# Two chunks' key sums on GpSimd, one tile turned by DMA, and new lists for the first stage of a two-layer linear-attention kernel

## The chip, the cores and the metric

The kernel runs on one core of one Trainium2 chip. The metric is the device time of one execution in microseconds; it is compared as the median of several runs. All times below are microseconds unless marked ns.

## The reference

The input x has 2048 tokens of 512 features, in bfloat16. Two layers are applied; each is an attention block and an MLP block, both with a residual, and both layers use the same weights.

```python
def _A_ref(x, wqkv, wo):                       # 32 heads of 16 features
    q, k, v = qkv[0], qkv[1], qkv[2]           # from x @ wqkv
    phi = lambda t: jnp.where(t > 0, t + 1, jnp.exp(t)) + 1e-6
    pq, pk = phi(q), phi(k)
    kv = jnp.einsum("bhsd,bhse->bhde", pk, v)
    z = jnp.einsum("bhsd->bhd", pk)
    num = jnp.einsum("bhqd,bhde->bhqe", pq, kv)
    den = jnp.einsum("bhqd,bhd->bhq", pq, z)[..., None] + 1e-6
    return (num / den) ... @ wo
def _B_ref(x, w1, b1, w2, b2):                 # 512 -> 1792 -> 512
    return gelu(layernorm(x) @ w1 + b1) @ w2 + b2
x = x + _A_ref(_layernorm(x), A_wqkv, A_wo)
x = x + _B_ref(_layernorm(x), ...)             # and both once more
```

The change concerns z, the sum of phi(K) over all tokens, in the first layer.

## The kernel before

The 2048 tokens are 16 tiles of 128 tokens, numbered 0 to 15, in 4 chunks of 4 tiles. Names end in layer and tile (K0_14: layer one, tile 14) or in layer, chunk and part (Q0_3_2). The program makes a graph of named operations, and each of the five engines executes its own written list of names (CONF, ORDER: "pe" is TensorE, "act" ScalarE, "dve" VectorE, "pool" GpSimd, "sp" the queue that issues most DMAs). A planner walks through these lists with a cost for each operation; it gives out the buffers and PSUM banks in the order in which it sees operations start, and from that the program sets its semaphore waits. It does not change the order within a list. WAY, a second table, says for many operations on which engine or in which form they run.

The first stage of layer one takes the chunks in the order 3, 0, 1, 2. For each tile it does the following.

- Layer norm. statsA0 and aggrA0 (VectorE, L742, L744) give mean and variance; vepsA0 (mostly GpSimd, L755) and powA0 (GpSimd, L757) give rstd; nmrA0 (GpSimd, L774) is made for those tiles whose normA0 runs on ScalarE (L777); the other normA0 run on VectorE (L782). The tiles of chunk 3 are only centred (cenA0) and are scaled later (yscA0).
- Transposition. TA0 is a DMA transpose that SP issues (L792). Tiles 1, 12, 13, 14 and 15 are turned on TensorE instead (PTA0, L805), and ScalarE copies the result out of PSUM (tcA0, L815).
- K0 (TensorE, L860), then phi: expk0 and reluk0 (ScalarE, L830, L841), mink0 (VectorE, L834 or L843), phik0 (VectorE, L836 or L847; phik0_6 on GpSimd). Where the table says "max", there is no relu and phik0 reads PSUM itself.
- Q0 (L878, L891) with the same phi.
- G0 (L961): normed tile transposed times phi(K), summed over all 16 tiles in PSUM banks 0 to 3. K, Q, the PTA0, Z and D operations share banks 4 to 7 meanwhile.

z is made by attn_z. With ZC=(0, 3), layer one makes it on TensorE: for each chunk, Z0_c multiplies each of the 16 blocks of phi(K) by one column of ones (L942), and VectorE adds the result to zs (zs0_c, L948, L951). In layer two, whose entry is 3, three chunks go another way that the function also holds: tiles are added into zacc in float32 on GpSimd or VectorE (za1, L914), the sum is split into a high and a low bfloat16 part (zhi, zlo), and one block of eight one-column matmuls sums over the partitions (ZH, L930), from which zsh writes zs:

```python
            if n < cf["ZC"][L]:
                ...
                    on_pool = eng(f"za{L}_{st}") != "dve"
                    G.op("pool" if on_pool else "dve",
                         lambda e, second=second, k=k: e.tensor_tensor(
                             zacc[:], pkb[:, zfirst[L].slot, :] if second else zacc[:], pkb[:, pks[k].slot, :], op=ALU.add),
```

After the stage, zb0 puts zs on a block-diagonal mask, D0_c_k (L1085) makes the denominators, ln and rec (ScalarE, L1087, L1089) their reciprocals and pr0 (L1093) the products; for chunks 2 and 3 this is done by token (ZR0, cpz0, pz0, red0, den0, rec0, pr0). cpg0 copies G out of PSUM, KV0 (L1016) and kvm0 (L1035) make the masked product with wv, M0 (L1039) multiplies by wo, cpm0 copies, and WO0 (L1109) makes the attention's output. RA0 adds the residual; normB0, TB0 or PTB0 lead to the MLP, whose matmuls are W10 (L1141) and W20 (L1180).

GpSimd also issues the loads of the later weights (wv, wo, w1_0, w1_1, w2_0, w2_1, L682), which wait for all transposes of the stage. SP loads the biases b1 and b2; b1 is turned by a small DMA transpose (Tb1, L1239) and copied by ScalarE (b1c, L1240) for the gelu.

## Time and profile before

| | |
|---|---|
| median of 3 runs | 325.48 |
| lowest and highest | 325.1 and 325.51 |
| the profiled execution | 325.25 |
| its span in the trace | 323.5 |
| TensorE matmul, busy | 318.4 |
| VectorE, busy | 216.5 |
| ScalarE, busy | 195.0 |
| GpSimd, busy | 134.8 |
| granted TensorE clock | 1.0 |

The span is the time in the trace from the first to the last instruction; the device time of the same execution is 1.75 longer. In the page's strips, the span is cut into 40 slices of 8.1 each, and a digit is the busy share in tenths. In a timeline a row is: start, duration, engine, line, operation, output<-input, count, and in brackets the idle time before it. PEld is the weight load, which overlaps PE. The chain of waits puts 91% of the span on TensorE.

### The profile page before, as it was taken

Reading aid. Unit: us, or ns where it says so; the run is one execution under the profiler, and the core shown is the slowest. Engines: PE = TensorE matmul, PEld = TensorE weight load, DVE = VectorE, ACT = ScalarE, POOL = GpSimd, SP = SyncE. Lnnn points to the kernel's source line nnn. Section 1 sums busy time; section 2 is a strip of 40 time slices with the busy share of each in tenths; the row PEclk is TensorE's granted clock in tenths of the full one; section 3 lists DMA queues with packets and bytes.
Section 4 is the critical chain, followed back from the end, with each engine's and each line's share of the span. In section 5 each row is a group of like instructions: output and inputs, shape, how many; then the busy total and the mean of one; then the engine's idle time right before and its main releaser. Section 6 shows DMA issues by size and latency. Waiting matters only on the chain.

```text
span 323.5 us, 4765 instructions
## 1 busy us (share of the span) xinstructions
PE 318.4 (98%) x1698; PEld 159.9 (49%) x1729; DVE 216.5 (67%) x506; ACT 195.0 (60%) x336; POOL 134.8 (42%) x224
## 2 busy tenths in 40 slices
PE   8999999999999999999999999999999999999996
...
POOL 4673268638703359000266645763541754000000
...
DMA packets 47028, 20.39 MB, mean 63 GB/s; under 512 B 42076, under 2 KB 45532, under 8 KB 47004
## 3 DMA queue, kind: packets, MB, share of 16 engines
...
q8 instruction: 14, 0.23, 0.3%
q14 instruction: 10, 0.08, 0.1%
...
## 4 chain that ended last, share of the span: by engine, by line
PE 91%; DVE 7%; issue 1%
PE ps L1180 28%; PE ps L1141 26%; PE ps L860 8%; PE ps L1109 6%; PE ps L878 5%; PE ps L993 4%; PE ps L961 4%; PE ps L891 3%; DVE xsb L1114 2%; DVE stats L742 2%; PE ps L698 2%; DVE yb L782 1%; PE ps L1167 1%; DVE lr L1061 1%; PE ps L1085 1%; DVE rd L1064 1%
## 5 line engine op out<-in xcount | busy, mean ns | idle before, releaser
L1147 ACT ACTIVATE gT<-ps,b1c 128x512 bf16<-128x512 f32 (+1 forms) x140 | 77.0, 600 | 63.3 <-PE ps L1141 62.6
L1141 PE MATMUL ps<-t,w 128*128 128x512 bf16 (+1 forms) x556 | 101.2, 336 | 0.2
L1180 PE MATMUL ps<-w,gT 128*128 128x512 bf16 x424 | 97.6, 379 | 0.5
L1141 PEld LDWEIGHTS ps<-t,w 128*128 128x128 bf16 x560 | 54.7, 98 | 43.8 <-ACT t L815 0.3
L1180 PEld LDWEIGHTS ps<-w,gT 128*128 128x128 bf16 x434 | 42.5, 98 | 50.0
L757 POOL TENSOR_TENSOR rstd<-veps,neghalf 128x1 f32<-128x1 f32 x64 | 38.5, 612 | 5.2 <-DVE veps L755 3.1
L830 ACT ACTIVATE eb<-ps 128x512 bf16<-128x512 f32 x56 | 32.4, 600 | 13.1 <-PE ps L878 6.2
L1190 DVE TENSOR_TENSOR pkb<-ps,xsb 128x512 bf16<-128x512 f32 x15 | 10.1, 684 | 40.7 <-PE ps L1180 40.7
L742 DVE BATCH_NORM_STATS2 stats<-xsb 128x6 f32<-128x512 f32 x48 | 32.2, 677 | 0.3
L860 PE MATMUL ps<-wqkv,t 128*128 128x512 bf16 x125 | 31.1, 379 | 0.2
L1109 PE MATMUL ps<-gtb,t 128*128 128x512 bf16 x123 | 30.1, 379 | 0.3
L841 ACT ACTIVATE rb<-ps 128x512 bf16<-128x512 f32 x38 | 22.2, 601 | 8.9 <-PE ps L860 6.7
L747 POOL TENSOR_SCALAR veps<-mv 128x1 f32<-128x1 f32 x32 | 8.7, 272 | 44.6 <-DVE mv L744 42.2
L755 POOL TENSOR_SCALAR veps<-mv 128x1 f32<-128x1 f32 x28 | 7.2, 262 | 45.1 <-DVE mv L744 43.7
L777 ACT ACTIVATE yb<-xsb,nmr,rstd 128x512 bf16<-128x512 f32 x21 | 16.9, 810 | 11.6 <-POOL nmr L774 11.5
L782 DVE TENSOR_SCALAR yb<-xsb,mv,rstd 128x512 bf16<-128x512 f32 x27 | 14.8, 559 | 11.4 <-POOL rstd L757 11.2
L1186 DVE TENSOR_TENSOR xsb<-ps,xsb 128x512 f32<-128x512 f32 x16 | 10.9, 682 | 16.8 <-PE ps L1180 14.3
L843 DVE TENSOR_SCALAR eb<-eb 128x512 bf16<-128x512 bf16 x46 | 14.5, 329 | 7.8 <-ACT eb L830 7.6
L860 PEld LDWEIGHTS ps<-wqkv,t 128*128 128x128 bf16 x128 | 12.4, 98 | 14.6 <-ACT eb L830 0.3
L878 PE MATMUL ps<-wqkv,t 128*128 128x512 bf16 x76 | 19.4, 379 | 0.2
L1109 PEld LDWEIGHTS ps<-gtb,t 128*128 128x128 bf16 x128 | 12.4, 98 | 14.2 <-ACT gtb L974 0.5
L1126 POOL TENSOR_TENSOR xsb<-xsb,b2b 128x512 f32<-128x512 f32 x14 | 17.3, 1235 | 1.0 <-DVE yb L782 0.7
...
## 6 DMA issues: line engine op xcount, KB each, us to landing
...
t<-yb SPq DMA_TRANSPOSE x56, 2.5
...
t<-t SPq DMA_TRANSPOSE x20, 2.4
```

The source lines that it names most:

```text
L742: G.op("dve", lambda e: e.bn_stats(stats[:, s.slot, :], src()), 602, reads=src_keys, writes=[k + "s"], tiles=[s, *src_tiles], prio=prio, n ...
L757: G.op("pool", lambda e: e.tensor_tensor(rstd[:, s.slot:s.slot + 1], veps[:, s.slot:s.slot + 1], neghalf[:], op=ALU.pow), 530, reads=[k + ...
L782: G.op("dve", lambda e: e.tensor_scalar(yb[:, y.slot, :], src(), stats[:, s.slot, 2:3] if by_act else mv[:, s.slot, 0:1], rstd[:, s.slot:s ...
L830: G.op("act", lambda e: e.activation(eb[:, et.slot, :], bank(bt), ACT.Exp, scale=factor()), 569 if by else 483, reads=[src_key, *more], wr ...
L841: G.op("act", lambda e: e.activation(rb[:, rt.slot, :], bank(bt), ACT.Relu, scale=factor()), 569 if by else 478, reads=[src_key, *more], w ...
L860: ins = e.matmul(bank(b), lhsT=yTa(yT)[:, dt, k * P:(k + 1) * P], rhs=wqkv[:, dt, D:2 * D], start=(dt == 0), stop=(dt == DT - 1))
L878: ins = e.matmul(bank(b), lhsT=yTa(yT)[:, dt, k * P:(k + 1) * P], rhs=wqkv[:, dt, 0:D], start=(dt == 0), stop=(dt == DT - 1))
L1109: ins = e.matmul(bank(wb), lhsT=yTa(pq)[:, kt, k * P:(k + 1) * P], rhs=gtb[:, kt, :], start=(kt == 0), stop=(kt == DT - 1))
L1126: G.op("pool" if on_pool else "dve", lambda e: e.tensor_tensor(xsb[:, st, :], xsb[:, st, :], b2b[:], op=ALU.add), 1120 if on_pool else 600 ...
L1141: ins = e.matmul(bank(b, n), lhsT=w1[:, dt, ft * P:(ft + 1) * P], rhs=yTa(yT)[:, dt, k0 * P:k1 * P], start=(dt == 0), stop=(dt == DT - 1))
L1147: G.op("act", lambda e, ft=ft, b=b, k0=k0, k1=k1, n=n: e.activation(gT[:, g.slot, ft * 512 + k0 * P:ft * 512 + k1 * P], bank(b, n), ACT.Ge ...
L1180: ins = e.matmul(bank(b), lhsT=gT[:, g.slot, ft * 512 + k * P:ft * 512 + (k + 1) * P], rhs=w2[:, ft, :], start=(ft == 0), stop=(ft == FT - 1))
```

## The change

ZC becomes (2, 3): the first two chunks of layer one (chunks 3 and 0) take the other way through attn_z. Z0_3, Z0_0, zs0_3 and zs0_0 go; za0_13, za0_14, za0_15, za0_0, za0_1, za0_2, za0_3 (all on GpSimd, since the table does not name them), zhi0, zlo0, ZH0 and zsh0 come. Tile 1 of layer one is turned by DMA: PTA0_1 and tcA0_1 go, TA0_1 comes. The lists of all five engines are re-ordered between their first few operations and the first MLP of chunk 0, and are the same as before from there on: from W10_0_12_1 in TensorE's list, reluq0_2_2 in ScalarE's, aggrB0_6 in VectorE's, pz0_2_1 in GpSimd's, TB0_2 in SP's. One line more in a list moves the line numbers of the functions by one.

```diff
-    C0=(3, 0, 1, 2), N_WARM=8, ZC=(0, 3), LQ='sp', N_HALF=1, N_K=4, N_Q=3, P_Z0=6.15, N_PB=1, N_PT=8, P_DEN=-50.43,
+    C0=(3, 0, 1, 2), N_WARM=8, ZC=(2, 3), LQ='sp', N_HALF=1, N_K=4, N_Q=3, P_Z0=6.15, N_PB=1, N_PT=8, P_DEN=-50.43,
...
         "pe":
-            "warm PTA0_12 idle0_0 PTA0_13 K0_12 idle0_1 K0_13 PTA0_14 Q0_3_0 Q0_3_2 PTA0_15 G0_12_0 K0_14 K0_15 "
-            "Q0_3_3 Q0_3_1 G0_13_0 PTA0_1 G0_14_0 K0_0 Z0_3 G0_15_0 K0_1 K0_3 K0_2 Q0_0_2 Q0_0_3 G0_0_0 G0_1_0 Q0_0_0 "
-            "K0_8 G0_2_0 G0_3_0 K0_5 Z0_0 K0_4 K0_6 K0_7 Q0_0_1 K0_10 K0_11 Q0_1_0 K0_9 Q0_1_3 Z0_1 G0_4_0 Z0_2 "
-            "Q0_1_2 Q0_1_1 G0_5_0 D0_0_3 D0_0_0 G0_6_0 D0_0_1 G0_7_0 D0_0_2 G0_8_0 ZR0 G0_9_0 G0_10_0 G0_11_0 G0_11_2 "
-            "D0_1_0 G0_11_1 Q0_2_0 G0_11_3 KV0_0 D0_1_1 KV0_1 D0_1_2 KV0_2 KV0_3 Q0_2_1 M0_1 M0_2 M0_0 M0_3 Q0_2_2 "
-            "WO0_0_0 WO0_0_1 WO0_0_2 WO0_0_3 D0_1_3 WO0_1_0 WO0_3_0 WO0_2_0 Q0_2_3 WO0_5_0 WO0_4_0 WO0_6_0 PTB0_0 "
...
+            "warm PTA0_12 idle0_0 PTA0_13 K0_12 idle0_1 K0_13 PTA0_14 Q0_3_0 K0_14 PTA0_15 G0_12_0 Q0_3_2 K0_15 "
+            "Q0_3_3 G0_13_0 Q0_3_1 K0_0 G0_14_0 K0_3 G0_15_0 K0_1 G0_0_0 Q0_0_2 K0_2 Q0_0_3 Q0_0_1 G0_1_0 Q0_0_0 "
+            "G0_2_0 K0_8 K0_4 G0_3_0 K0_6 K0_5 K0_10 K0_7 G0_4_0 ZH0 K0_11 K0_9 Q0_1_3 Z0_1 Q0_1_0 Q0_1_1 Z0_2 G0_5_0 "
+            "Q0_1_2 D0_0_0 G0_6_0 G0_7_0 D0_0_1 D0_0_3 G0_8_0 D0_0_2 G0_9_0 G0_10_0 G0_11_0 G0_11_2 G0_11_1 D0_1_0 "
+            "Q0_2_0 G0_11_3 ZR0 D0_1_1 KV0_0 KV0_1 KV0_2 KV0_3 D0_1_2 D0_1_3 M0_2 M0_0 M0_3 M0_1 Q0_2_1 WO0_0_0 "
+            "WO0_0_1 WO0_0_2 WO0_0_3 WO0_1_0 WO0_2_0 Q0_2_2 WO0_3_0 WO0_5_0 WO0_6_0 Q0_2_3 PTB0_0 WO0_7_0 WO0_4_0 "
...
         "act":
-            "wk1 sumA0_13 tcA0_12 sqA0_13 tcA0_13 expk0_12 reluk0_12 tcA0_14 expk0_13 reluq0_3_0 reluk0_13 tcA0_15 "
-            "reluq0_3_2 expq0_3_0 expk0_14 reluk0_14 normA0_3 expq0_3_2 expk0_15 reluk0_15 reluq0_3_3 tcA0_1 yscA0_15 "
-            "expk0_0 expq0_3_3 reluq0_3_1 expq0_3_1 reluk0_1 expk0_1 normA0_5 normA0_8 expk0_2 reluq0_0_2 normA0_10 "
-            "reluk0_3 expq0_0_3 expk0_3 normA0_6 normA0_7 expk0_8 expq0_0_0 expq0_0_2 reluq0_0_0 reluk0_5 expk0_5 "
-            "expk0_4 normA0_9 reluk0_6 expk0_6 expk0_7 reluq0_0_1 expq0_0_1 expk0_10 expk0_11 reluk0_11 expk0_9 "
-            "reluk0_9 expq0_1_3 expq0_1_2 expq0_1_0 reluq0_1_2 expq0_1_1 ln0_0_0 rec0_0_0 ln0_0_1 rec0_0_1 ln0_0_3 "
-            "rec0_0_3 reluq0_1_1 cpz0 ln0_0_2 rec0_0_2 ln0_1_0 expq0_2_0 rec0_1_0 ln0_1_1 b1c rec0_1_1 cpm0_1 cpm0_0 "
-            "cpm0_3 ln0_1_2 rec0_1_2 ln0_1_3 rec0_1_3 expq0_2_1 expq0_2_3 reluq0_2_1 reluq0_2_3 expq0_2_2 tcB0_0 "
...
+            "wk1 sumA0_13 tcA0_12 sqA0_13 tcA0_13 expk0_12 reluk0_12 tcA0_14 reluk0_13 expk0_13 reluq0_3_0 tcA0_15 "
+            "expq0_3_0 reluk0_14 expk0_14 normA0_3 expq0_3_3 reluq0_3_3 expk0_15 yscA0_15 reluk0_15 expk0_0 "
+            "reluq0_3_2 expq0_3_2 expq0_3_1 normA0_10 reluq0_3_1 expk0_1 reluk0_1 normA0_8 reluk0_3 expk0_3 expk0_2 "
+            "reluq0_0_2 expq0_0_2 normA0_5 normA0_6 expq0_0_3 expq0_0_0 reluq0_0_0 normA0_7 expk0_8 reluq0_0_1 "
+            "expq0_0_1 expk0_4 normA0_9 expk0_6 reluk0_6 expk0_5 reluk0_5 expk0_7 expk0_10 expk0_11 reluk0_11 expk0_9 "
+            "reluk0_9 expq0_1_3 b1c expq0_1_0 expq0_1_1 ln0_0_0 expq0_1_2 rec0_0_0 reluq0_1_2 ln0_0_1 ln0_0_3 "
+            "rec0_0_1 rec0_0_3 reluq0_1_1 ln0_0_2 rec0_0_2 ln0_1_0 expq0_2_0 rec0_1_0 ln0_1_1 cpz0 rec0_1_1 cpm0_0 "
+            "cpm0_1 cpm0_3 ln0_1_2 rec0_1_2 ln0_1_3 rec0_1_3 expq0_2_1 reluq0_2_1 expq0_2_2 expq0_2_3 tcB0_0 "
+            "reluq0_2_3 gelu0_0_5_0 gelu0_0_8_0 gelu0_0_11_0 gelu0_0_0_0 gelu0_0_13_0 gelu0_0_12_0 gelu0_0_2_0 "
...
         "dve":
-            "statsA0_15 mink0_12 aggrA0_15 phik0_12 vepsA0_14 cenA0_15 statsA0_0 aggrA0_0 vepsA0_15 statsA0_3 "
-            "mink0_13 statsA0_1 aggrA0_3 normA0_0 phik0_13 statsA0_2 aggrA0_1 aggrA0_2 mink0_14 yscA0_13 statsA0_10 "
-            "normA0_1 yscA0_14 phik0_14 normA0_2 minq0_3_0 mink0_15 statsA0_5 phik0_15 phiq0_3_0 aggrA0_5 aggrA0_10 "
-            "minq0_3_2 statsA0_8 zs0_3 phiq0_3_2 aggrA0_8 mink0_0 statsA0_6 statsA0_4 statsA0_7 aggrA0_4 aggrA0_7 "
-            "aggrA0_6 phik0_0 statsA0_9 mink0_1 minq0_3_3 aggrA0_9 mink0_2 phik0_1 phik0_2 minq0_3_1 normA0_4 "
-            "statsA0_11 minq0_0_3 mink0_3 phiq0_3_3 phiq0_0_3 phik0_3 aggrA0_11 phiq0_3_1 mink0_8 phik0_8 minq0_0_0 "
-            "phiq0_0_0 normA0_11 mink0_5 mink0_4 zs0_0 phik0_5 phik0_4 mink0_7 minq0_0_2 mink0_6 phiq0_0_2 phik0_7 "
-            "mink0_10 mink0_11 phik0_10 minq0_0_1 mink0_9 phik0_11 phik0_9 zs0_1 minq0_1_3 zs0_2 zb0 phiq0_1_3 "
-            "phiq0_0_1 dz0 minq0_1_0 minq0_1_2 phiq0_1_0 pr0_0_0 minq0_1_1 pr0_0_1 pr0_0_3 cpg0_0 cpg0_1 cpg0_2 "
-            "cpg0_3 minq0_2_0 kvm0_2 kvm0_1 kvm0_0 kvm0_3 phiq0_2_0 cpm0_2 pz0_2_0 red0_2_0 RA0_0 statsB0_0 RA0_1 "
-            "statsB0_1 aggrB0_0 aggrB0_1 RA0_2 RA0_3 normB0_1 statsB0_2 normB0_0 RA0_4 aggrB0_2 statsB0_3 pz0_3_3 "
-            "den0_2_0 RA0_5 aggrB0_3 normB0_2 red0_3_3 rec0_2_0 normB0_3 RA0_6 pz0_3_1 pz0_3_0 pr0_2_0 minq0_2_3 "
...
+            "statsA0_15 mink0_12 aggrA0_15 phik0_12 vepsA0_14 cenA0_15 vepsA0_15 statsA0_3 statsA0_0 aggrA0_3 "
+            "aggrA0_0 statsA0_2 mink0_13 yscA0_14 phik0_13 normA0_0 yscA0_13 statsA0_1 aggrA0_1 mink0_14 aggrA0_2 "
+            "statsA0_10 phik0_14 normA0_1 minq0_3_0 aggrA0_10 statsA0_8 aggrA0_8 normA0_2 mink0_15 minq0_3_3 phik0_15 "
+            "phiq0_3_0 statsA0_5 mink0_0 aggrA0_5 phik0_0 statsA0_7 phiq0_3_3 statsA0_6 statsA0_4 aggrA0_7 aggrA0_4 "
+            "aggrA0_6 mink0_1 minq0_3_1 phik0_1 statsA0_11 phiq0_3_1 minq0_3_2 mink0_2 aggrA0_11 normA0_4 phik0_2 "
+            "statsA0_9 phiq0_3_2 mink0_3 aggrA0_9 minq0_0_3 phiq0_0_3 minq0_0_2 minq0_0_0 phik0_3 phiq0_0_2 mink0_8 "
+            "normA0_11 phik0_8 minq0_0_1 mink0_4 phiq0_0_1 zhi0 phik0_4 phiq0_0_0 zlo0 mink0_5 mink0_7 phik0_5 "
+            "mink0_6 zsh0 phik0_7 mink0_10 phik0_10 mink0_11 phik0_11 mink0_9 phik0_9 zs0_1 minq0_1_0 zs0_2 phiq0_1_0 "
+            "zb0 minq0_1_3 phiq0_1_3 dz0 minq0_1_1 pr0_0_0 minq0_1_2 pr0_0_1 pr0_0_3 cpg0_0 cpg0_2 cpg0_1 cpg0_3 "
+            "minq0_2_0 kvm0_2 kvm0_0 kvm0_3 kvm0_1 phiq0_2_0 cpm0_2 pz0_2_0 red0_2_0 RA0_0 RA0_1 statsB0_0 statsB0_1 "
+            "aggrB0_0 aggrB0_1 RA0_2 RA0_3 normB0_1 RA0_5 normB0_0 den0_2_0 statsB0_2 statsB0_3 aggrB0_2 rec0_2_0 "
...
         "pool":
-            "id0 bdm0 neghalf id1 bdm1 powA0_12 vepsA0_13 eps6 powA0_13 powA0_14 vepsA0_0 powA0_15 b1z powA0_0 "
-            "vepsA0_3 powA0_3 nmrA0_3 vepsA0_1 powA0_1 vepsA0_2 powA0_2 vepsA0_5 powA0_5 nmrA0_5 vepsA0_8 powA0_8 "
-            "vepsA0_10 powA0_10 nmrA0_10 nmrA0_8 vepsA0_7 vepsA0_4 powA0_7 powA0_4 vepsA0_9 vepsA0_6 powA0_6 powA0_9 "
-            "nmrA0_7 nmrA0_6 vepsA0_11 powA0_11 nmrA0_9 phik0_6 w1_1 phiq0_1_2 wv wo w2_1 phiq0_1_1 w1_0 pr0_0_2 "
-            "pr0_1_0 pr0_1_1 w2_0 pr0_1_2 pr0_1_3 vepsB0_1 powB0_1 vepsB0_0 powB0_0 b20_0 vepsB0_2 powB0_2 vepsB0_3 "
...
+            "id0 bdm0 neghalf id1 bdm1 powA0_12 vepsA0_13 eps6 powA0_13 b1z powA0_15 powA0_14 vepsA0_3 vepsA0_0 "
+            "powA0_0 powA0_3 nmrA0_3 za0_13 vepsA0_1 vepsA0_2 powA0_1 powA0_2 za0_14 vepsA0_10 vepsA0_8 powA0_10 "
+            "powA0_8 nmrA0_8 nmrA0_10 vepsA0_5 za0_15 powA0_5 za0_0 vepsA0_7 vepsA0_4 vepsA0_6 powA0_4 powA0_6 "
+            "nmrA0_5 nmrA0_6 za0_1 powA0_7 vepsA0_11 nmrA0_7 vepsA0_9 powA0_9 powA0_11 za0_2 nmrA0_9 za0_3 phik0_6 wv "
+            "w1_1 wo w1_0 w2_0 w2_1 phiq0_1_2 phiq0_1_1 pr0_0_2 pr0_1_0 pr0_1_1 pr0_1_2 pr0_1_3 vepsB0_1 powB0_1 "
+            "vepsB0_0 powB0_0 vepsB0_2 powB0_2 vepsB0_3 powB0_3 phiq0_2_3 b20_0 pz0_2_1 vepsB0_6 vepsB0_7 vepsB0_5 "
...
         "sp":
-            "x0 x1 wk0 x2 wq xc0 xc1 xc2 TA0_0 TA0_3 TA0_2 TA0_5 TA0_8 TA0_4 TA0_6 TA0_7 TA0_10 TA0_11 TA0_9 b1 b2 "
-            "Tb1 TB0_1 TB0_2 TB0_3 TP0_2_0 TB0_5 TB0_7 TB0_6 TB0_4 TP0_3_1 TP0_3_0 TP0_3_3 TP0_2_3 TP0_2_1 TP0_2_2 "
...
+            "x0 x1 wk0 x2 wq xc0 xc1 xc2 TA0_0 TA0_3 TA0_1 TA0_2 TA0_10 TA0_8 b1 TA0_4 TA0_6 TA0_5 TA0_7 TA0_11 TA0_9 "
+            "Tb1 TB0_1 b2 TB0_2 TB0_3 TP0_2_0 TB0_5 TB0_7 TB0_6 TB0_4 TP0_3_1 TP0_3_0 TP0_3_3 TP0_2_3 TP0_2_1 TP0_2_2 "
...
-        "TA0_0": "dma", "TA0_1": "pe", "TA0_10": "dma", "TA0_11": "dma", "TA0_12": "pe", "TA0_13": "pe", "TA0_14": "pe",
+        "TA0_0": "dma", "TA0_1": "dma", "TA0_10": "dma", "TA0_11": "dma", "TA0_12": "pe", "TA0_13": "pe", "TA0_14": "pe",
```

98 rows, old and new, of the table ORDER are left out of this document.

## Prediction

> **What bounds the kernel now.** I read the page first, then the PE timeline of the first stage, then the rows of what is removed and added.
>
> ```profile
> PE 318.4 (98%) x1698; PEld 159.9 (49%) x1729; DVE 216.5 (67%) x506; ACT 195.0 (60%) x336; POOL 134.8 (42%) x224
> ...
> PE   8999999999999999999999999999999999999996
> ...
> POOL 4673268638703359000266645763541754000000
> ```
>
> TensorE is busy from the second slice to the last. Busy includes pipelined waiting, so I also took the ends of the operations from the trace's semaphore posts: the n-th post of an engine belongs to the n-th name of its list. From 7 us on, posts follow each other at 0.864 us for four 512-column matmuls, and only G0_15 shows more (0.04 us). So any TensorE work taken out shortens the run, and any new wait lengthens it, microsecond for microsecond.
>
> ```profile
> 16.59 1.03 PE L860 MATMUL ps<-wqkv,t 128*128 128x512 bf16 x4
> 17.45 0.54 PE L942 MATMUL ps<-onesm,pkb 128*128 128x1 bf16 x16
> 18.09 0.81 PE L961 MATMUL ps<-pkb,yb 128*128 128x512 bf16 x3
> ```
>
> This is Z0_3, one of the two blocks to go, between K0_0 and G0_15: sixteen one-column matmuls.
>
> **What is removed and added on TensorE.** Z0_3 and Z0_0 post 0.38 us after their predecessors and push the next post by 0.02: 2 x 0.40 = 0.80 us. The transpose PTA0_1 is 0.22. ZH0 comes in; its twin ZH1 posts after 0.18 and pushes the next by 0.02: 0.20. Sum: 0.80 + 0.22 - 0.20 = 0.82 us less, if TensorE stays filled. Nothing hides this work today, so all of it counts. tcA0_1 (ScalarE, 0.48) goes too.
>
> **What GpSimd gets: seven adds.** Their rows are those of layer two's (L914):
>
> ```profile
> L914 POOL TENSOR_TENSOR zacc<-zacc,pkb x6: 1152/1248/1534, 166.0 to 187.1; 128x512 f32<-128x512 f32 x6
> L914 DVE TENSOR_TENSOR zacc<-zacc,pkb x4: 679/683/692, 165.3 to 174.1; 128x512 f32<-128x512 f32 x4
> ```
>
> 7 x 1.15 = 8.1 us at least, 8.7 at the median, put between the small operations that make rstd. GpSimd is busy 14.35 of the 27.5 us from 6.5 to 34, so it fits in sum. But each add stands before a nmr or pow that a norm waits for, and it holds VectorE:
>
> ```profile
> 34.14 1.26 POOL L847 TENSOR_TENSOR pkb<-eb,rb 128x512 bf16<-128x512 bf16 x1 [5.44 <-DVE eb L843]
> ```
> ```profile
> 35.05 0.50 DVE L834 TENSOR_SCALAR eb<-eb 128x512 bf16<-128x512 bf16 x1
> 35.65 0.29 DVE L843 TENSOR_SCALAR eb<-eb 128x512 bf16<-128x512 bf16 x1
> ```
>
> The short VectorE operation that starts at 35.05, inside the 1.26 us GpSimd add, ends 0.15 after the add does (35.40); the next one takes 0.29. So such an operation is held until the add ends. Statistics and operations that read PSUM are not held. Each add can cost VectorE between nothing and about 1.1 us.
>
> The Trainium skill (GPSIMD Engine Reference, Engine selection and Key points) speaks against this edit: it puts elementwise work on VectorE and says that GpSimd shares its memory interfaces with VectorE. The two L914 rows agree (1.248 against 0.683). If sharing only doubled a VectorE operation's time, 0.28 would be lost at each add instead of up to 1.1, and the sum below would come to about -0.6; the row at 35.05 shows a hold, so I use holds.
>
> **Where the adds bite, list by list.** TensorE starts on time if its operand is posted 0.24 before the previous post (G0_15 today has 0.19 and loses 0.04). Other lags from the posts: VectorE to GpSimd 0.13, GpSimd to VectorE 0.12, GpSimd to ScalarE 0.15, TensorE to ScalarE 0.14.
>
> First chain, to G0_15. cenA0_15 posts at 9.60 as now; vepsA0_15 9.66; powA0_15 +0.67; powA0_14 +0.53; vepsA0_3, vepsA0_0 to 11.45; powA0_0 +0.65; powA0_3 +0.53; nmrA0_3 +0.37 = 13.00; za0_13 +1.12 = 14.12. mink0_14 is held to 14.27; aggrA0_2 14.36; vepsA0_2 14.69; powA0_1 +0.65; powA0_2 +0.53; za0_14 +1.15 = 17.02. normA0_2 is held to 17.30; mink0_15, minq0_3_3, phik0_15 (0.20 + 0.20 + 0.33) = 18.03. With the new list TensorE comes to G0_15 at 18.28: wait 0. It has no slack left, though. phik0_0 follows at +1.82 (0.33 + 0.60 + 0.20 + 0.09 + 0.60) = 19.85 and is wanted 0.24 before 20.01: wait 0.08.
>
> Second chain, ScalarE. normA0_10, normA0_5 and normA0_9 stand in its list where their nmr, now behind a za, comes at 19.28, 24.80 and 30.40. ScalarE is free at 19.29, 24.83 and 30.48, so each wait is about 0.1. Adding 0.57 (scaled) or 0.49 for each exp or relu and 0.70 for each norm, expk0_3 posts at 23.36 (Q0_0_1 waits 0.06), reluq0_0_0 at 27.82 (K0_4 waits 0.14), reluk0_6 at 32.23 (K0_7 waits 0.09): PSUM banks 4 to 7 rotate among all of K and Q, and these posts free them.
>
> Third, the end of the sum. za0_3 ends at 31.55 and holds minq0_0_1 to 31.70; mink0_4, phiq0_0_1, zhi0, phik0_4 (0.20 + 0.33 + 0.34 + 0.60) = 33.17: G0_4 waits 0.07. phiq0_0_0 and zlo0 (0.93): ZH0 waits 0.07.
>
> Fourth, a wait that has nothing to do with GpSimd: M0_2 now stands two D matmuls (0.43) behind KV0_3, where Q0_2_1 (0.86) stood too. kvm0_2 posts 0.32 after KV0_3, and 0.24 more makes 0.56: wait 0.13. Then pr0_1_3 on GpSimd and normB0_0 before PTB0_0, 0 to 0.2, taken 0.05, because today's margin there is 0.36 and the new list shortens it.
>
> Sum of waits: 0.08 + 0.29 + 0.14 + 0.13 + 0.05 = 0.69. **Net -0.82 + 0.69 = -0.13 us.**
>
> Bounds. These waits are links of one 25 us chain. If it runs 2% quicker (0.5 us) than my roundings, all but 0.18 go; a chain this tight could also leave less than that. On the other side, small GpSimd operations are themselves slowed when VectorE runs beside them: powA0_3 today takes 0.91 from vepsA0_3 where 0.65 is usual, during phik0_13. Twice that, 0.5, and the median instead of the minimum for the adds (4 of 7 on the chain, 0.1 each, 0.4) make waits of 1.6, so +0.8.
>
> **Edits at nothing.** TA0_1 goes to the SP queue as a twelfth transpose: 1.2 us of issue, 2.55 to landing (12.41 to 14.95 for TA0_0). normA0_1 posts near 15.7, so it lands near 18.3; K0_1 starts at 19.1. Behind it, TA0_2 waits for normA0_2 (17.30) anyway. Cover: 0.8 us. The six weight loads now leave GpSimd back to back (0.8 to 0.95 us each) after phik0_6, ahead of phiq0_1_2, which is needed only near 43; wv is wanted at 48. b2 behind TB0_1 costs SP 0.4 us while the queue is empty.
>
> **Rivals.**
>
> *The lists close.* All operands come in time: -0.82 + 0.1 = 324.75. For it: today's list, equally tight, loses 0.04. Against: the seven holds are not there today.
>
> *GpSimd is the bound of the stage.* Every add is lengthened and small operations pile up behind: waits 1.6, time 326.3. It decides from the point where nmrA0_3 posts later than about 13.4, since the rest follows in series. For it: the zero slack at G0_15 and the 0.91 above.
>
> *Tb1 blocks ScalarE.* b1c moves from 50.6 to behind expq0_1_3, near 37.8, and everything for D0 stands behind it. Its transpose Tb1 waits for TA0_9 (lands about 34.6).
>
> ```profile
> t<-yb SPq DMA_TRANSPOSE x56, 2.5
> ...
> b1t<-b1r SPq DMA_TRANSPOSE x1, 6.7
> ```
>
> At 2.5 it lands at 37.2, in time. At the 6.7 of today's row, 41.4: ScalarE stands 3.6 us and TensorE some 3.4, time 328.7. Today Tb1 was issued at 35.56, beside w1_1 (35.44), whose packets came first on the engines; in the new order wv leaves about 1.5 us after Tb1. The Trainium skill (Trainium Kernel Development and Optimization, Key Constraints) says that all queues share the same 16 DMA engines; the row fits. It decides if Tb1 lands after 37.9.
>
> *The removed work was only filler.* If the Z blocks covered late operands, the gain is 0 and the new waits remain: 325.48 + 0.5 = 326.0. Against: everything else is dense.
>
> **How the numbers follow.** The profiled execution took 325.25 (323.5 span and 1.75 around it); the median is 325.48, 0.23 above. 325.25 - 0.13 + 0.23 = 325.35, my forecast. A measurement of this kernel can tell about 0.2%, 0.65 us. Forecast (waits 0.2 to 1.4) 0.50; lists close (waits under 0.17) 0.27; GpSimd bound 0.13; Tb1 0.05; filler 0.05. Faster by over 0.2% comes from the second case and a little of the first: 0.29. Slower: 0.10 of the third, all of Tb1, and 0.06 from the upper tails of the forecast and of the filler: 0.21. The rest, 0.50, lies within. The range goes from the closed lists to the GpSimd case: 324.7 to 326.4; the likeliest case alone 324.9 to 326.1.
>
> **What would show it.** In the trace after: TensorE posts of G0_15, G0_0, Q0_0_1, K0_4, K0_7, G0_4, ZH0 and M0_2 later than 0.864 by the waits above, D0_0_0 posting near 41.6; nmrA0_3 near 13.0; VectorE operations of 0.4 to 1.1 us inside the za rows; b1t landing before 37.9. A gain of over 0.65 us would say that holds are shorter than I take them; a loss of over 0.65 that the chain on GpSimd is longer, or Tb1 late. A change after W10 starts would be outside all this.

## The result and the profile after

The changed kernel takes 326.62 us (median of 8 runs, 325.82 to 327.5) against 325.13 for the kernel before on the same chip (median of 8). The ratio is 1.0043, 95% interval 1.0033 to 1.0053: slower by 0.43%, some 1.4 us. The forecast was 325.35 with a range of 324.7 to 326.4; the median lies above it. The forecast started from 325.48, the median of three runs of the kernel before; eight runs give 325.13, so by luck its starting point stood 0.35 nearer to the result. The profiled execution took 327.5 (span 325.8), 0.9 above the median.

The page of the changed kernel: the lines that answer to those of before, and its chain of waits, the work that ended last, followed back from the end:

```profile
PE 320.7 (98%) x1701; PEld 157.7 (48%) x1701; DVE 220.7 (68%) x507; ACT 194.5 (60%) x335; POOL 142.3 (44%) x231
...
PE   8999999999999999999999999999999999999996
...
POOL 4799546448703259000367645863541754000000
...
PE 81%; DVE 8%; POOL 4%; DMA 3%; issue 2%; ACT 1%; SPq 0%
```

TensorE's strip looks the same, and its busy time has grown by 2.3 us although 0.82 us of work was taken out: busy includes pipelined waiting. The chain says more. Before, it read:

```profile
PE 91%; DVE 7%; issue 1%
```

There it left TensorE once, for VectorE, from 53.8 to 77.3 us. In the changed kernel it leaves TensorE twice. From 204.8 to 229.1 us it runs over VectorE and a DMA transpose to the product WO1_12, whose wait shows in this profile alone (see below), so that part of the fall to 81% is not typical. The other stretch ends at 33.5 us, in the changed stage, and runs over GpSimd for most of 11 to 26 us (start, duration, engine, tile, line):

```profile
11.78 1.53 POOL rstd L758 x2
...
13.67 1.11 POOL zacc L915
...
18.00 1.37 POOL rstd L758 x2
...
29.98 1.17 POOL zacc L915
...
31.23 0.43 POOL nmr L775
...
32.89 0.59 ACT rb L842
```

These are pow, sum and nmr on GpSimd, and at the end reluk0_6 on ScalarE, for which K0_7 waits. The waits of TensorE that the profile itself names:

```profile
PE ps L1142 <- issue: 0.6, 1, 0.6
PE ps L861 <- ACT rb L842: 0.5, 2, 0.2
PE ps L1110 <- DMA t<-t: 0.4, 1, 0.4
```

Columns: who waited for whom, us in total, times, longest. L861 is K0, in the changed stage. L1110 (WO1_12) and L1142 (W11_2_4) lie at 229 and 279 us, in lists that the edit does not touch.

The ledger, from the semaphore posts as in the prediction (time beyond an operation's own length), profiled execution against profiled execution:

| | us |
|---|---|
| work taken out | -0.82 |
| first chain: K0_0, K0_3, G0_15, G0_0 (0.05, 0.04, 0.13, 0.13) less the 0.04 of before | +0.31 |
| second chain: Q0_0_1, K0_4, K0_7 (0.30, 0.41, 0.39) | +1.10 |
| third: G0_4, ZH0 (0.06, 0.05) | +0.11 |
| fourth: M0_2 | +0.13 |
| W11_2_4 | +0.73 |
| WO1_12 | +0.57 |
| first 13 us (K0_15 posts at 13.28 instead of 13.09) | +0.19 |
| sum | 2.32 |
| last post, 323.28 against 320.95 | 2.33 |

Sixteen profiles were taken, one each of the two kernels and of the fourteen variants below. The wait at WO1_12 shows in this one alone, and the first 13 us vary by 0.7 from profile to profile (K0_15 posts between 12.81 and 13.52); these two, 0.76, are most of what this execution has over the median. Without them the ledger gives 1.56, and the medians differ by 1.49.

The sums themselves on GpSimd, and VectorE's operations beside two of them (start, duration, engine, line, operation):

```profile
L915 POOL TENSOR_TENSOR zacc<-zacc,pkb x12: 1152/1158/1539, 16.3 to 188.1; 128x512 f32<-128x512 f32 x12
L915 POOL TENSOR_TENSOR zacc<-pkb x2: 1150/1152/1153, 13.6 to 165.1; 128x512 f32<-128x512 bf16 x2
```
```profile
13.63 1.15 POOL L915 TENSOR_TENSOR zacc<-pkb 128x512 f32<-128x512 bf16 x1
...
14.00 0.93 DVE L844 TENSOR_SCALAR eb<-eb 128x512 bf16<-128x512 bf16 x1
...
29.98 1.16 POOL L915 TENSOR_TENSOR zacc<-zacc,pkb 128x512 f32<-128x512 f32 x1
...
29.98 1.30 DVE L835 TENSOR_SCALAR eb<-eb 128x512 bf16<-128x512 bf16 x1
```

mink0_14 and mink0_8, 0.2 us of work each, end 0.15 and 0.14 after the sum beside them does. The Trainium skill (SBUF — State Buffer, Who interferes with whom) calls the port pair of the two engines an exclusive lock, held for a whole instruction; these rows agree.

How full the engines are in the stage, from the windows view at 13 to 40 us (27 us long; columns: window, length, then busy us and instructions of PE, PEld, DVE, ACT, POOL, granted clock, DMA share, GB/s). Before:

```profile
13.00:40.00 27.00, 26.80 (x183) 13.06 (x185) 23.25 (x74) 23.95 (x45) 12.83 (x30) 1.00 0.38 89
```
After:
```profile
13.00:40.00 27.00, 26.42 (x141) 10.95 (x139) 26.42 (x72) 24.51 (x45) 22.42 (x40) 1.00 0.34 65
```

GpSimd went from 12.83 to 22.42 and VectorE from 23.25 to 26.42, that is 98%. Neither bounded the stage before; which of them does now is the question of the experiments.

### The profile page after: what moved, and what is told of

Same layout as the page of the kernel before. It is cut to its first block, busy times and chain, and to the rows that moved or that the text cites. A ratio compares the mean times of both kernels' runs of the same rounds, so it can differ in the third digit from the quotient of the medians.

```text
span 325.8 us, 4751 instructions
## 1 busy us (share of the span) xinstructions
PE 320.7 (98%) x1701; PEld 157.7 (48%) x1701; DVE 220.7 (68%) x507; ACT 194.5 (60%) x335; POOL 142.3 (44%) x231
## 4 chain that ended last, share of the span: by engine, by line
PE 81%; DVE 8%; POOL 4%; DMA 3%; issue 2%; ACT 1%; SPq 0%
PE ps L1181 29%; PE ps L1142 27%; PE ps L1110 6%; PE ps L861 5%; PE ps L994 4%; PE ps L879 3%; PE ps L962 2%; PE ps L892 2%; POOL rstd L758 2%; DVE stats L743 2%; DMA t<-t 2%; DMA t<-in_A_x_dram 1%; POOL zacc L915 1%; DVE xsb L1115 1%; PE ps L1168 1%
## 5 line engine op out<-in xcount | busy, mean ns | idle before, releaser
L1142 PE MATMUL ps<-t,w 128*128 128x512 bf16 (+1 forms) x560 | 101.5, 336 | 0.6 <-issue 0.6
L1142 PEld LDWEIGHTS ps<-t,w 128*128 128x128 bf16 x560 | 54.7, 98 | 44.5 <-ACT gT L1148 1.2
L758 POOL TENSOR_TENSOR rstd<-veps,neghalf 128x1 f32<-128x1 f32 x64 | 39.2, 624 | 5.2 <-DVE veps L756 3.5
L861 PE MATMUL ps<-wqkv,t 128*128 128x512 bf16 x128 | 31.9, 379 | 0.5 <-ACT rb L842 0.5
L1110 PE MATMUL ps<-gtb,t 128*128 128x512 bf16 x128 | 30.7, 379 | 0.4 <-DMA t<-t 0.4
L748 POOL TENSOR_SCALAR veps<-mv 128x1 f32<-128x1 f32 x32 | 8.0, 251 | 48.2 <-DVE mv L745 45.3
L756 POOL TENSOR_SCALAR veps<-mv 128x1 f32<-128x1 f32 x28 | 7.0, 270 | 41.1 <-DVE mv L745 40.2
L844 DVE TENSOR_SCALAR eb<-eb 128x512 bf16<-128x512 bf16 x46 | 15.7, 354 | 6.9 <-ACT eb L831 6.9
L879 PE MATMUL ps<-wqkv,t 128*128 128x512 bf16 x80 | 20.4, 379 | 0.0
L861 PEld LDWEIGHTS ps<-wqkv,t 128*128 128x128 bf16 x128 | 11.8, 98 | 16.2 <-ACT rb L842 2.2
L1110 PEld LDWEIGHTS ps<-gtb,t 128*128 128x128 bf16 x128 | 12.2, 98 | 15.0 <-ACT gtb L975 0.9
```

The lines of the kernel that those rows point to most:

```text
L758: G.op("pool", lambda e: e.tensor_tensor(rstd[:, s.slot:s.slot + 1], veps[:, s.slot:s.slot + 1], neghalf[:], op=ALU.pow), 530, reads=[k + ...
L861: ins = e.matmul(bank(b), lhsT=yTa(yT)[:, dt, k * P:(k + 1) * P], rhs=wqkv[:, dt, D:2 * D], start=(dt == 0), stop=(dt == DT - 1))
L879: ins = e.matmul(bank(b), lhsT=yTa(yT)[:, dt, k * P:(k + 1) * P], rhs=wqkv[:, dt, 0:D], start=(dt == 0), stop=(dt == DT - 1))
L1110: ins = e.matmul(bank(wb), lhsT=yTa(pq)[:, kt, k * P:(k + 1) * P], rhs=gtb[:, kt, :], start=(kt == 0), stop=(kt == DT - 1))
L1142: ins = e.matmul(bank(b, n), lhsT=w1[:, dt, ft * P:(ft + 1) * P], rhs=yTa(yT)[:, dt, k0 * P:k1 * P], start=(dt == 0), stop=(dt == DT - 1))
```

## The experiments

Theory A: the seven sums (za0) lengthen GpSimd's chain, so the nmr behind them, the norms on ScalarE and the PSUM banks come late. Rivals: the new lists by themselves (R1), the DMA transpose (R2), VectorE as the engine that is late (H), and, for W11_2_4, a part of the change against something else (R3, later F).

**e1: narrow sums.** Each sum adds 16 columns instead of 512; the rest of z of chunks 3 and 0 is left out.

```diff
-  zacc[:], pkb[:, zfirst[L].slot, :] if second else zacc[:], pkb[:, pks[k].slot, :], op=ALU.add)
+  zacc[:, 0:ZW[L]], ... pkb[:, pks[k].slot, 0:ZW[L]], op=ALU.add)      # ZW = (16, 512)
+  e.memset(zacc[:], 1.0)   # at the start, on VectorE
```

> The changed kernel with the seven sums of layer one 16 columns wide instead of 512 (most of z's sum of chunks 3 and 0 is left out; every instruction, wait and list stays). Theory A (the seven wide sums lengthen GpSimd's chain, so that normA0_3, _10, _5 and _9 on ScalarE and with them the PSUM banks come late): nmrA0_3 posts before 12.8, nmrA0_10 near 17, nmrA0_9 before 27; the extra TensorE time of G0_15, G0_0, Q0_0_1, K0_4, K0_7, G0_4 and ZH0 (1.5 us in sum) goes to under 0.2, M0_2 keeps its 0.13; time 1.2 to 1.5 below the changed kernel, 325.1 to 325.4. Rival R1 (the newly searched lists and their order of PSUM banks cost it, the sums do not): the same waits on TensorE, within 0.3 of the changed kernel's 326.6. Rival R3 (stalls after 200 us, WO1_12 and W11_2_4, are part of the change): they stay, and the time falls by less than the waits that go.

Measured: 325.93, ratio to before 1.0018 (1.0009 to 1.0027), so 0.8 below the changed kernel. Q0_0_1 kept 0.10 of its 0.30; K0_4, K0_7, G0_4 and ZH0 kept nothing; M0_2 kept 0.13; K0_0 rose to 0.17. Stage waits went from 1.69 to 0.44. nmrA0_9 posted at 29.59 instead of 31.67; all three figures that I had expected (12.8, 17 and 27 for nmrA0_3, nmrA0_10 and nmrA0_9) were too early: 14.05, 19.35 and 29.59. The chain of waits is TensorE's again:

```profile
PE 97%; DMA 1%; issue 1%; ACT 0%; DVE 0%
```

R1 falls: the same lists and banks lose little when the sums are short. R3 holds: W11_2_4 still waited 0.58. So this kernel, with nearly the whole cost of the sums gone, is still not faster than before: -0.82 + 0.40 + 0.58 makes +0.16, and its profile lost 0.43 more in the first 13 us (K0_15 at 13.52, the latest of the sixteen), ahead of every sum. Its median lies 0.60 above the kernel before; whether those 0.43 belong to this variant or to the one execution stays open, and with it why it gained less than the 1.2 that A expected at least.

**e2: tile 1 by DMA alone, in the kernel before.**

```diff
-"TA0_1": "pe"   ... PTA0_1 ... tcA0_1 ...
+"TA0_1": "dma"  # TA0_1 behind TA0_3 on SP; all other lists as before
```

> The kernel before with one part of the change alone: tile 1 of layer one turned by a DMA transpose (PTA0_1 and tcA0_1 gone, TA0_1 on SP behind TA0_3), all other lists as before. Theory A holds this part to be a gain: 0.22 of TensorE's work gone, K0_0 not later than its bank; time 0.1 to 0.3 below before, 324.85 to 325.05. Rival R2 (the DMA transpose lands late or delays the transposes queued behind it): TA0_1's data comes after 12.5, K0_0 starts late, time 0.2 or more above before.

Measured: 327.55, ratio 1.0069 (1.0057 to 1.0081), slower than the whole change. Neither side named the place. TensorE's waits in this kernel:

```profile
PE ps L1113 <- DVE xsb L1118: 1.6, 3, 0.8
```

They are WO0_2, WO0_6 and WO0_7 at 57 to 63 us (0.33, 0.98 and 0.86 by the posts), 45 us behind the edit. One PSUM buffer fewer, and the planner gave out the banks in another order, so that WO0_6 and WO0_7 needed banks that the residual additions (RA0) still held.

**e3: z of both chunks on TensorE again, in the changed kernel.**

```diff
-ZC=(2, 3)
+ZC=(0, 3)   # Z0_3 behind K0_3, Z0_0 behind K0_5, zs0_3 and zs0_0 on VectorE; za0, zhi0, zlo0, ZH0, zsh0 out
```

> The changed kernel with z of chunks 3 and 0 summed on TensorE again (Z0_3 behind K0_3 with zs0_3, Z0_0 behind K0_5 with zs0_0; the seven sums, ZH0 and its three vector operations gone), the other lists and the DMA transpose as in the changed kernel. Theory A: 0.80 of TensorE's work comes back, 0.20 goes, and 1.2 to 1.5 of waits go: 0.6 to 0.9 below the changed kernel, 325.7 to 326.0. Rival R1 (lists and banks): 0.6 above the changed kernel, 327.2.

Measured: 327.92, ratio 1.0074 (1.0062 to 1.0086); neither theory's figure. My places were bad (Z0_3 waited 0.76, K0_10 0.49), and the banks moved again (WO0_2 0.51, two W10 0.67). It says nothing on the sums. In the experiments behind e4 the banks are pinned, or the planner gives the same ones (in e9 and e14 but for K0_9 and K0_11).

**e4: the sums later in GpSimd's list.**

```diff
-nmrA0_3 za0_13 ... powA0_2 za0_14 ... nmrA0_10 vepsA0_5 za0_15 powA0_5 za0_0 ... nmrA0_6 za0_1 ... za0_2 nmrA0_9 za0_3
+nmrA0_3 ... powA0_2 za0_13 ... nmrA0_10 za0_14 ... nmrA0_6 za0_15 ... nmrA0_9 za0_0 za0_1 za0_2 za0_3
```

> The changed kernel with its seven sums moved later in GpSimd's list alone: za0_13 behind powA0_2, za0_14 behind nmrA0_10, za0_15 behind nmrA0_6, za0_0 to za0_3 behind nmrA0_9; every other list as it is. Theory A: nmrA0_10 near 17, nmrA0_5 near 23, nmrA0_9 near 28 instead of 19.98, 25.77, 31.67; the extra time of Q0_0_1, K0_4 and K0_7 (1.1 us) goes to under 0.4, za0_3 stays near 32.8, G0_4 and ZH0 keep 0.06 each; 0.6 to 0.9 below the changed kernel, 325.7 to 326.0. Rival R1: within 0.3 of it. Rival R4 (what counts is how much GpSimd and VectorE hinder each other, not the order): nmrA0_10 and the rest come earlier, but VectorE's evictions come later by as much, and the time stays.

Measured: 329.34, ratio 1.0120 (1.0107 to 1.0133); no theory's figure. The first half of A came true: nmrA0_10, nmrA0_5 and nmrA0_9 posted at 18.71, 24.61 and 29.25, and Q0_0_1, K0_4 and K0_7 waited 0.10, 0 and 0. But za0_3 ended at 34.35, zhi0 stood at the head of VectorE's queue for it, phik0_4 behind zhi0, and G0_4 waited 2.4 us. TensorE then ran at half clock for 3.4 us, which made G0_4 itself longer by 0.46, K0_11 by 0.86 and K0_9 by 0.45; all timed executions of this kernel show the lower mean clock of 0.995. The planner gave out other banks too, but only from ZH0 on, behind G0_4's wait. The rows (the windows view at 36 to 38 us; the chain's wait):

```profile
36.00:38.00 2.00, 2.00 (x14) 0.73 (x12) 2.00 (x8) 0.63 (x2) 0.52 (x1) 0.52 0.00 0
```
```profile
PE ps L963 <- DVE pkb L838: 2.4, 1, 2.4
```

**e5: TensorE's instruction stream shifted.** A queue named instruction moves packets of 16 KB (13 of them, 0.21 MB, in the changed kernel). I took them for TensorE's program, fetched piece by piece; this run, which changes nothing but TensorE's list, moves them. In the changed kernel one starts at 273.08, when SP issues TB1_10, TB1_8 and TB1_11, on which W11_2_4 depends.

```diff
-idle("warm", [D] * cf["N_WARM"] + [P] * cf["N_WARM2"])
+idle("warm", [170] * (3 * cf["N_WARM"]) + [P] * cf["N_WARM2"])
```

> The changed kernel with the eight warm-up matmuls of 512 columns cut into twenty-four of 170, so that TensorE's instruction stream is 16 matmuls and weight loads longer ahead of 5 us and every later 16 KB packet of the queue named instruction falls some 3.4 us earlier against the work; nothing else changes. Theory F (in the changed kernel the packet at 273.08 falls on the transposes TB1_10, TB1_8 and TB1_11, which then take 4.95 us together instead of 3.82, and W11_2_4 waits 0.73 for them): packet near 269.6, the three transposes 3.8 us, no wait at W11_2_4, time 0.5 to 0.7 below the changed kernel, 325.9 to 326.1. Rival B (the wait comes from the PSUM bank of that product, 0 here and 1 before): the wait stays, 326.6.

Measured: 326.01, ratio 1.0023 (1.0013 to 1.0034), 0.6 below the changed kernel. The packet started at 268.67 and W11_2_4 did not wait. SP's queue in the timeline (start, duration of the issues, count) and the DMA view from 272 to 277 us (its instruction queue, and the transposes with the us from issue to landing); first the changed kernel, then e5:

```profile
273.00 4.95 SPq L793 DMA_TRANSPOSE t<-yb  x3
```
```profile
q8 instruction: 1, 0.02, 1.5%
...
t<-yb SPq DMA_TRANSPOSE x4, 3.1
```
```profile
272.90 3.81 SPq L793 DMA_TRANSPOSE t<-yb  x3
```
```profile
t<-yb SPq DMA_TRANSPOSE x4, 2.5
```

The first of the three issues takes 2.33 us with the packet and 1.19 without. The last of the three lands at 277.93 instead of 279.17; in the changed kernel W11_2_4 starts at 279.26, right behind that. The bank (0 in both) is not the cause, so B falls. The price was paid in part elsewhere: another packet, now at 16.68, fell on TA0_1, whose issue took 2.21 instead of 1.19, and K0_1 waited 0.42; K1_15 and W11_1_3 waited 0.34 and 0.25. This profiled execution, 326.66, is the longest of its eight, so these waits need not stand in the median.

**e6: e2 with the banks of the kernel before.**

```diff
-for b in allowed:
+for b in ((BANK[t.name],) if t.name in BANK else allowed):   # BANK: each buffer's bank in the kernel before
```

> The kernel before with tile 1 of layer one by DMA alone, and each PSUM bank pinned to the one that it has in the kernel before. Theory B2 (the 2.2 us that the same edit cost with free banks came from other banks: WO0_5 to WO0_7 waited 1.9 us for the additions of RA0): no wait at WO0_2 to WO0_7, time 0 to 0.3 below before, 325.0 to 325.3. Rival R2 (the transpose itself costs): 0.5 or more above before, waits at G0_14 and K0_8 over 0.3.

Measured: 325.54, ratio 1.0008 (0.9999 to 1.0017). No wait at any WO0, so 2.0 of e2's 2.2 us were the banks. B2 holds in its waits, though its time (325.0 to 325.3) was too low. The 0.22 of work saved did not appear either: G0_14 waited 0.14 and K0_8 0.11.

**e7: ScalarE's order.**

```diff
-normA0_10 reluq0_3_1 expk0_1 reluk0_1 normA0_8 reluk0_3 expk0_3 ... normA0_5 normA0_6 expq0_0_3 ... normA0_9 expk0_6 reluk0_6
+reluq0_3_1 expk0_1 reluk0_1 reluk0_3 expk0_3 normA0_10 normA0_8 ... expq0_0_3 normA0_5 normA0_6 ... expk0_6 reluk0_6 normA0_9
```

> The changed kernel with ScalarE's list alone moved so that no normalization stands ahead of work that is ready: reluk0_3 and expk0_3 ahead of normA0_10 and normA0_8, expq0_0_3 ahead of normA0_5, expk0_6 and reluk0_6 ahead of normA0_9; PSUM banks as in the changed kernel. Theory A (GpSimd's late nmrA0_10, nmrA0_5 and nmrA0_9 hold ScalarE, which holds the banks of Q0_0_1, K0_4 and K0_7): expk0_3 near 22.4 instead of 24.05, reluk0_6 near 32 instead of 33.48, the 1.10 of extra time at the three falls to 0.3 or less, time 0.7 to 0.9 below the changed kernel, 325.7 to 325.9. Rival (VectorE, not ScalarE, holds those banks): extra time and time stay within 0.2.

Measured: 326.81, ratio 1.0048 (1.0034 to 1.0062), no gain: A's 325.7 to 325.9 failed, and the rival's time held. expk0_3 came at 22.35 as planned and Q0_0_1 lost its wait. Then expq0_0_3, moved ahead, waited for a buffer that phik0_2 (VectorE, 25.79) frees, and reluq0_0_0 posted at 28.80 instead of 28.77: K0_4 waited 1.02. So behind ScalarE's wait for nmrA0_5 there stands a second path, through VectorE, that is nearly as late: a better order on ScalarE alone gains nothing.

**e8: e7, e5's shift, and D0_1_1 behind KV0_3 as cover for M0_2.**

```diff
-ZR0 D0_1_1 KV0_0 KV0_1 KV0_2 KV0_3 D0_1_2 D0_1_3 M0_2
+ZR0 KV0_0 KV0_1 KV0_2 KV0_3 D0_1_1 D0_1_2 D0_1_3 M0_2     # with e5's warm-up and e7's order; banks pinned as in e7
```

> ScalarE's order of e7, the warm-up cut of e5, and D0_1_1 behind KV0_3, so that three products instead of two cover kvm0_2 ahead of M0_2; banks as in the changed kernel. If the three losses are separate they add: 0.8 + 0.6 + 0.1 below the changed kernel, 325.0 to 325.2, the same as the kernel before within 0.2. If they are one loss seen twice, or TensorE is then held by something else, 325.7 or more.

Measured: 327.33, ratio 1.0064 (1.0051 to 1.0076). W11_2_4 and M0_2 waited no more, but KV0_3, M0_3, M0_1, WO0_0_1 and WO0_5 now waited 0.15, 0.17, 0.20, 0.20 and 0.53. These five show neither in e5 nor in e7, so they go with the moved D0_1_1: to take 0.13 of wait at M0_2 cost 1.25 behind it.

**e9: e4's order, and the sum read later.**

```diff
-phiq0_0_1 zhi0 phik0_4 phiq0_0_0 zlo0 ... mink0_6 zsh0 phik0_7          # VectorE
+phiq0_0_1 phik0_4 phiq0_0_0 ... mink0_6 zhi0 phik0_7 zlo0 ... phik0_11 zsh0
-G0_4_0 ZH0 K0_11 K0_9 Q0_1_3                                            # TensorE
+G0_4_0 K0_11 K0_9 Q0_1_3 ZH0                                            # warm: [204] * 20
```

> e4's order (the seven sums behind the normalizations' small operations on GpSimd), and now also their use later: zhi0 behind mink0_6, zlo0 behind phik0_7, zsh0 behind phik0_11 on VectorE, ZH0 behind Q0_1_3 on TensorE; the warm-up cut into twenty pieces of 204 columns, 12 matmuls more than in the changed kernel. Theory A, with e4's 2.90, 0.86 and 0.45 at G0_4, K0_11 and K0_9 put down to zhi0, which waited for za0_3 at the head of VectorE's queue: those three under 0.3 in sum, no wait at W11_2_4, about 0.4 of other waits, so 0.4 to 0.6 below before, 324.7 to 324.9. Rival H (the sums hold VectorE wherever they stand, 0.5 to 1.0 us each time): K0_11, K0_9 and Q0_1_x wait 0.8 or more in sum, time at or above before, 325.3 to 326.

Measured: 326.44, ratio 1.0042 (1.0028 to 1.0057). Up to K0_9 theory A had all it wanted: K0_9 posts at 35.76, 0.82 earlier than in the kernel before, with only ZH0's 0.20 still to come. Then Q0_1_3 (L898) and others lost it:

```profile
PE ps L898 <- DVE pkb L843: 0.7, 1, 0.7
PE ps L898 <- DVE eb L850: 0.3, 1, 0.3
```

Q0_1_3, Z0_1, Q0_1_0 and Q0_1_1 posted 2.9 us late together in the profile, of which 1.7 are a half clock from 38.88 to 42.30 that only this one of its six timed executions shows (327.79; the others 325.97 to 326.63). za0_1 to za0_3 held phiq0_0_1 and mink0_5 for 1.0 each. Rival H was right about this order, though the time lies above its range (325.3 to 326) too.

**e10: the sums on VectorE.**

```diff
-WAY={
+WAY={"za0_13": "dve", "za0_14": "dve", "za0_15": "dve", "za0_0": "dve", "za0_1": "dve", "za0_2": "dve", "za0_3": "dve",   # and the seven names moved to VectorE's list, banks pinned
```

> The changed kernel with the seven sums on VectorE instead of GpSimd, each behind a later phi(K) in its list; banks as in the changed kernel. It adds seven operations of some 0.6 us (4.2 us) to VectorE and takes away the seven sums of 1.1 us from GpSimd, and with them the times that VectorE's operations are held inside them. Theory A (GpSimd's chain is what is late): nmrA0_9 by 30, normA waits gone. Theory H (VectorE's queue is what frees ScalarE's buffers and the banks; the holds cost it about 3.5 us by 33 us): VectorE is as late as in the changed kernel or later, the waits of K0_4 and K0_7 stay near 0.8 in sum or grow, time within 0.5 of the changed kernel or above it. If GpSimd alone counted, 325.4 or less.

Measured: 327.23, ratio 1.0068 (1.0055 to 1.0081). As H expected, it is slower: G0_0, Q0_0_0 and K0_4 waited 0.73, 0.69 and 0.82. The window from 13 to 40 us:

```profile
13.00:40.00 27.00, 25.16 (x135) 10.82 (x136) 26.79 (x76) 23.88 (x43) 15.00 (x31) 1.00 0.34 63
```

VectorE is busy for 26.79 us of it, and GpSimd, with 7.4 us less to do than in the changed kernel (15.00 against 22.42), still posted nmrA0_9 at 31.44, since it waited for VectorE's aggr. Relieving GpSimd at VectorE's cost moves the late engine; it does not remove the lateness.

**e11: VectorE relieved, GpSimd as it is.**

```diff
-e.bn_stats(stats[:, s.slot, :], src())
+e.bn_stats(stats[:, s.slot, :], src()[:, 0:64] if tag in NARROW else src())   # NARROW: tiles 4 to 11 of layer one; 448 of their 512 columns are left out
```

> The changed kernel with the statistics of tiles 4 to 11 of layer one taken from 64 of the 512 columns (the other columns are left out); the seven wide sums, every list, wait and bank stay. It takes some 4 us of work from VectorE between 13 and 32 us and nothing from GpSimd. Theory H (VectorE's queue, 98% busy from 13 to 40 us because of the holds inside the sums, is what frees the buffers and banks): VectorE under 90% busy there, zs0_1 posts by 38.7 instead of 39.82, the extra time of Q0_0_1, K0_4 and K0_7 under 0.4 in sum (1.10 in the changed kernel), W11_2_4 still waits 0.6 to 0.7; 0.8 to 1.3 below the changed kernel, 325.3 to 325.8. Theory A (GpSimd's own chain, full of the sums, is what is late): nmrA0_9 still after 31, those waits stay at 0.8 or more, 326.2 to 326.6.

Measured: 327.17, ratio 1.0052 (1.0038 to 1.0065): as slow as the changed kernel. VectorE had 24.35 us of work instead of 26.42, and now it waits itself:

```profile
DVE eb L845 <- ACT eb L832: 1.4, 1, 1.4
DVE yb L784 <- POOL rstd L759: 0.6, 1, 0.6
```

nmrA0_9 posts at 32.30, and G0_15, Q0_0_1, K0_4 and K0_7 wait 0.32, 0.81, 0.29 and 0.39. The time lies above both ranges, but the sign is clear: VectorE was busy for 2.07 us less and brought nothing forward (zs0_1 posts at 40.45 instead of 39.82). In the order of the changed kernel it is GpSimd's chain that is late, as A says; H is refuted for this order.

**e12: a smaller shift of the stream.**

```diff
+idle("warm", [341] * 12 + [P] * cf["N_WARM2"])
```

> The changed kernel with the warm-up matmuls cut into twelve of 341 columns, 4 matmuls and weight loads more instead of e5's 16. Theory F: the instruction packet of TensorE moves by some 0.9 us only, to about 272.2, still on the transposes before W11_2_4; the wait there stays at 0.5 or more, and the time within 0.2 of the changed kernel, 326.4 to 326.8. If cutting the warm-up by itself was e5's gain: 326.0.

Measured: 326.53, ratio 1.0038 (1.0025 to 1.0051): the time that F expected, for another reason. The packet moved by 2.6 us, not 0.9, to 270.50; it missed the transposes and W11_2_4 did not wait. Two other packets hit: at 18.12 beside TA0_1 and TA0_2, and at 183.19 in a row of seven transposes. TA0_1 was issued in the usual 1.19 but landed 4.15 after the start of its issue instead of 2.41. K0_1 waited 1.24 by the posts and K1_15 0.71:

```profile
PE ps L861 <- DMA t<-yb: 1.6, 2, 1.1
```

Cutting the warm-up by itself therefore gains nothing; where the packets fall is what counts, and I could not foretell it to a microsecond.

**e13 and e14: e9 with the sums where GpSimd stood idle.** In e9, GpSimd waited 1.0 us for aggrA0_7 ahead of vepsA0_7, while za0_15 came three microseconds later.

```diff
-powA0_5 vepsA0_7 ... nmrA0_6 za0_15 powA0_7 ... nmrA0_9 za0_0 za0_1 za0_2 za0_3      # e9
+powA0_5 za0_15 vepsA0_7 ... nmrA0_6 za0_0 powA0_7 ... nmrA0_9 za0_1 za0_2 za0_3      # e14 and e13
+phik0_7 zhi0 mink0_10 zlo0 ... mink0_11 zsh0                    # VectorE, e13 alone; ZH0 behind Z0_1, banks pinned
```

> e9 with za0_15 ahead of vepsA0_7 (where GpSimd stood idle in e9) and za0_0 behind nmrA0_6, so that za0_3 ends 1.1 us earlier, near 33.4; zhi0 behind phik0_7, zlo0 behind mink0_10, zsh0 behind mink0_11 and ZH0 behind Z0_1, so that phik0_7, for which Q0_1_3 waited, comes 0.3 us earlier. Theory O (the place of the sums is what costs): Q0_1_3, Z0_1, Q0_1_0 and Q0_1_1 wait under 0.5 in sum, 0.2 to 0.5 below before, 324.8 to 325.1. Theory C (GpSimd and VectorE have no room for the sums, the wait moves once more): 0.8 or more of waits between G0_15 and G0_5, time 325.6 or more.

> e9 with only za0_15 ahead of vepsA0_7 and za0_0 behind nmrA0_6. Theory O: za0_3 near 33.4 instead of 34.56, mink0_5 no longer held to 34.71, Q0_1_3 waits under 0.4 instead of 0.85; 0.6 to 1.0 below e9, 325.3 to 325.7. Theory C: within 0.3 of e9, 326.1 to 326.7.

Measured: e13 325.59, ratio 1.0012 (1.0003 to 1.0020); e14 325.57, ratio 1.0020 (1.0008 to 1.0033). e14 came out as O has it: za0_3 ended at 33.20, Q0_1_3 waited 0.13, and it is 0.9 below e9. It is 0.7 below the changed kernel by the ratios, about as much as e5's shift alone gave, though its waits in the stage are 1.13 (Z0_1 0.37 and Q0_1_0 0.25 the largest) against 1.69. Its ledger: -0.82 + 1.13 - 0.04 = +0.27, and its last post is 0.26 later than in the kernel before. e13 came out as C has it: Q0_1_3 and Z0_1 waited no more, but ZH0 waited 0.33, Q0_1_0 0.35, Q0_0_2 0.21 and K0_4 0.24, 1.34 in the stage. So to move two of the sums into a stretch where GpSimd stood idle was worth 0.9 against e9. Against the changed kernel's own order with the packet moved (e5, 1.0023) nothing clear is gained (1.0020): the waits moved from order to order. No version that I ran beats the kernel before.

The packet and the wait at W11_2_4 in the sixteen profiles: with a packet of TensorE's stream starting within 0.2 us of the first of the three issues (the changed kernel, e1, e4, e7, e10, e11), that issue took 2.17 to 2.43 us and W11_2_4 waited 0.57 to 0.83; with none there (the kernel before and the nine others), it took 1.19 or 1.20 and nothing waited. The six share one TensorE list length; the kernel before has a longer one and its packet at 264.15. This holds for that issue alone. At 22 other transposes in these profiles a packet also started within 0.2 us of the issue, and they took anything from 1.19 to 2.40 us, eight of them at most 1.29. In the kernel before, too, packets fell 0.66 and 0.59 into two issues (at 237.74 and 263.56), which took 2.33 and 2.04, and no product waited. What a packet costs therefore depends on the place and on the slack behind it.

## Why the prediction was wrong

- Work taken out. 0.82 us: right, since the ledgers of the changed kernel and of e14 close within 0.01 with it. The part of it that comes from tile 1 brought nothing alone (e6).
- First chain. I had vepsA0_15 9.66, nmrA0_3 13.00, za0_14 17.02, phik0_15 18.03; the posts are 9.92, 13.68, 17.52 and 18.44. 0.26 of it is there at the start; powA0_0 and powA0_3 took 0.81 and 0.79 instead of 0.65 and 0.53, which adds the rest. Taken 0.08, measured 0.35 (with K0_0 and K0_3; 0.31 more than before). The zero slack at G0_15 that the prediction noted was used up.
- Second chain, the step that failed. I took nmrA0_10, nmrA0_5 and nmrA0_9 at 19.28, 24.80 and 30.40, just when ScalarE is free; they came at 19.98, 25.77 and 31.67. The waits were 0.30, 0.41 and 0.39 at the operations named, against 0.06, 0.14 and 0.09: a term of 0.29 was 1.10. The mechanism (sum, nmr, norm, exp or relu, bank, TensorE) is the predicted one, and e1 and e4 show it: with the sums short, or behind the nmr, these waits fall to 0.10, 0 and 0. The size was wrong in the main because I gave the pows their quick intervals, 0.65 for the first and 0.53 for the next, from post to post; powA0_0, powA0_3, powA0_10, powA0_5, powA0_6 and powA0_7 took 0.81, 0.79, 0.90, 0.71, 0.77 and 0.69. The twelve from powA0_0 to powA0_11, all ahead of nmrA0_9, took 7.93 in sum; with 0.65 (seven times) and 0.53 (five times) they make 7.20. The chain was 0.26 late at its start and 1.27 at nmrA0_9, so these 0.73 are most of the 1.01 that it lost on the way; the rest I did not resolve. The rows of the pows in the stage from 8 to 34 us, before and after (count, busy us, mean ns):

```profile
L757 POOL TENSOR_TENSOR rstd<-veps,neghalf 128x1 f32<-128x1 f32 x14 | 8.5, 610 | 2.5 <-DVE veps L755 1.9
```
```profile
L758 POOL TENSOR_TENSOR rstd<-veps,neghalf 128x1 f32<-128x1 f32 x14 | 8.9, 651 | 2.5 <-DVE veps L756 2.3
```

  Fourteen pows at 41 ns more are 0.57 us. The wide sums are not the main reason for that: in e1, with narrow ones, the mean is still 636 ns, powA0_0 and powA0_3 took 0.81 and 0.80 as well, and powA0_10 fell to 0.56. What else slowed them was not tested. The prediction had named this cost (0.5, from a pow of 0.91) and put it into the bounds instead of the sum. It also left out the second path through VectorE, which e7 laid open.
- Third and fourth. G0_4 0.06 (0.07), ZH0 0.05 (0.07), M0_2 0.13 (0.13), all as taken; PTB0_0 none (0.05 taken).
- The holds. mink0_14 and mink0_8 ended 0.15 and 0.14 after the sums: right. In e9, e13 and e14 phiq0_0_1 was held for 1.0 in the same way; that this is what keeps them from the full gain is likely but not tested.
- The rivals. "GpSimd is the bound of the stage" came closest, with its point of decision: nmrA0_3 later than 13.4, measured 13.68. It had a chance of 0.13 and waits of 1.6; they were 1.69. One part of it was wrong: the adds were not lengthened (1.11 to 1.15 from post to post, as taken), the small operations were. Tb1 did not block: b1c posts at 39.38, straight behind expq0_1_3 at 39.29. The lists did not close. "Only filler" falls with the ledgers, in which the 0.82 counts in full.
- The range, and a term put at nothing. The GpSimd rival's 326.3 would have held but for one sentence: "A change after W10 starts would be outside all this". It was not outside. Twenty-eight matmuls fewer in TensorE's list (two blocks of 16 and PTA0_1's 4 out, ZH0's 8 in) put a packet of instructions onto three transposes at 273 us, 220 us behind the edit, and W11_2_4 waited 0.73. With that packet moved (e5) the kernel takes 326.01. Together: from -0.13, the second chain adds 0.81, W11_2_4 0.73 and the first chain 0.23, and 0.08 that was taken for ZH0, G0_4 and PTB0_0 did not come. That makes +1.56; the medians say +1.49.

What stays open: what sets the moment at which a packet is fetched (4 more matmuls moved it by 2.6 us, 16 by 4.4; in the changed kernel 211 to 285 of TensorE's matmuls and weight loads lie between two packets, 253 on average), why the issue at 273 us is lengthened so much more than most others, and whether a fuller search could bring the stage's waits under 0.8 with the sums on GpSimd; apart from e1, e14's 1.13 is the least that I reached.
